# A third stream in chunks of 768 tokens, one product of 384 columns at a time, and a last product by token parity

## The chip, the cores and the metric

The kernel runs on one core of a Trainium2 chip. The metric is the device time of one execution in microseconds; of several runs, the median is taken.

## The reference, cut to what matters

Three layers follow each other over 8 batches of 576 tokens (4608 tokens, 512 features):

```python
# 1: attention with positive features, 8 heads of 64
proj = x @ w_phi; proj -= max(abs(proj)); phi = concat(exp(proj), exp(-proj))
out = (phi(q) @ (phi(k).T @ v)) / (phi(q) @ phi(k).sum() + 1e-6)
...
# 2: four experts, each a causal softmax attention over its batch; the two best per token are mixed
ye = softmax(scale * (x @ wq[e]) @ (x @ wk[e]).T, causal) @ (x @ wv[e]) @ wo[e]
...
# 3: mixing with the token before, then two products and a gate
xk = mu_k * x + (1 - mu_k) * x_prev;  xr = mu_r * x + (1 - mu_r) * x_prev
v = square(relu(xk @ w_k)) @ w_v
out = sigmoid(xr @ w_r) * v
```

`w_k` is 512 by 1024, `w_v` 1024 by 512, `w_r` 512 by 512.

## The kernel before

Everything is float32. Each product is made of three products of rounded parts (`mm3`: high by high, high by low, low by high), so that each operand has a `hi` and a `lo` tile (`split`, lines 94 to 99).

Work is written as streams (Python generators) of small tasks. `skewed` staggers the stages of successive tasks, and `weave` merges the streams by a clock of their own: the stream whose clock is lowest goes next, and a task adds its cost divided by the stream's rate. A task may have a condition; until it holds, the stream is passed over. The compiler's planner then orders the instructions of each engine by a simulated time and by priority; the streams `rk`, `compose` and `decodes` run at a lower priority (`-1000`) and so serve as filler.

- `favors` (first stream) is layer 1. For each of 160 pairs of token tiles it loads `raw`, splits it (`hi` on ScalarE, `lo` on GpSimd), makes `pj`, exponentials `ph`, the sums `kv`, the quotients `num`, and stores the result transposed in `XT`.
- `moe1` (second stream) is layer 2: `qk`, `vp`, scores `sc`, softmax `a`, transposes `at`, values `yp`. For each batch and pair of experts (`ep`) it stores its taps with `yd<-yt` (line 632). `stored[b]` is 2 when both pairs of a batch are issued.
- `compose` multiplies the output weights of layer 2 into `w_r` and `w_k` of layer 3 (12 blocks), so that layer 3's first products are taken straight from the taps; it leaves the weights in DRAM as `wf`. Products use even and odd tokens apart: a product of half tokens (`m`) serves both parities, and the products of slices 1 and 2 are added to it.
- `gates_keys` (third stream, `rk`) goes over the 4608 tokens in 9 chunks of `CH` = 512. A chunk loads its taps into `yc_` (one buffer, tag `y`), on ScalarE's queue; its condition is that the last batch that it touches is stored, that `compose` is done, and for the last two chunks that the second stream is over. Then 18 units follow: unit u has two products of 256 columns (12 matmuls) into one bank `rk`; every third one is copied to `m` by ScalarE, the others are added to `m` by VectorE into `z` (line 736) and stored to `kd`. Weights come as tiles `wt` of 512 KB, in three buffers, loaded on ScalarE's queue by `lw(n)`; after unit u the load for u+2 is issued. Until the first stream ends, all units share one bank; then two banks alternate.
- `moe2` (last product) goes over the same chunks: it loads pairs of blocks of `kd` (`kx`), applies relu and square, splits them into `XT` (free by then), and multiplies them with `w_v` into four banks `vacc` (24 matmuls of 512 columns per pair). `zs` is the gate (sigmoid). `fin` multiplies both into `o`, interleaving the two parities, and stores `out`. The first two `kx` have buffers of their own, the others lie in memory that the second stream frees when it ends.

When the second stream ends, a second `weave` (line 829) merges what is left of `rk` with `moe2`.

Of the kernel before, what the change touches and what calls it, by code (L numbers as in the profile page):

```python
# [13 lines left out]
P = 128  # L14
# [6 lines left out]
CH = 512  # L21
# [3 lines left out]
HC = CH // 2  # L25
NB = 18
# [48 lines left out]
def fused_kernel(ctx: ExitStack, tc: tile.TileContext, qT, kT, vx, wphi, wq, wk, wvg, wo, mu, w64, ident, cmask, tri, out):  # L75
# [12 lines left out]
    wf = [dram.tile([P, 2, 4, P], F32, name=f'wf{u}') for u in range(NB)]  # L88
    kd = [dram.tile([P, 12, CH], F32, name=f'kd{c}') for c in range(NC_)]

# [117 lines left out]
    def compose():  # L208
# [6 lines left out]
        for u in range(12):  # L215
            wth, wtl = (pR.tile([P, 4, 2, P], F32R, name=n, tag='w', bufs=3) for n in ('wth', 'wtl'))
            for hf in range(2):
                hz = (yield from decode(pF, 2 * u + hf, dict(tag='e', bufs=3), 2, 3, pool_raw=pR))
                ks = slice(2 * hf, 2 * hf + 2)
# [4 lines left out]
                split(wth[:, ks, 0], wtl[:, ks, 0], hz, 'a', nc.gpsimd)  # L224
                yield 1
                split(wth[:, ks, 1], wtl[:, ks, 1], a_, 'a', nc.gpsimd)
                yield 1
            ps = psK.tile([P, 512], F32, name='fo', tag='rk')
            for ep in range(2):
                es = slice(ep * P, ep * P + P)  # L230
                mm3(ps[:, ep * 256:ep * 256 + 256], [(sw[:, 0, kt, es], sw[:, 1, kt, es], wth[:, kt].rearrange('p x n -> p (x n)'), wtl[:, kt].rearrange('p x n -> p (x n)')) for kt in range(4)])
                yield 1
# [33 lines left out]
    def favor(b):  # L266
        kvbank = {}

        def proj_stages(src, g, u, dst, first=False):
# [98 lines left out]
        def q_unit(g, u):  # L368
# [17 lines left out]
            def num():  # L386
# [10 lines left out]
                dn = pF.tile([P, 2, 2], F32, name='dn', tag='dn', bufs=3)  # L397
                rd = pF.tile([P, 2, 2], F32, name='rd', tag='rd', bufs=3)
# [28 lines left out]
    def moe1():  # L427
# [168 lines left out]
        def av_task(b, e, hf):  # L596
# [72 lines left out]
    def favors():  # L669
# [17 lines left out]
        for f in range(8):  # L687
            s_ = pW.tile([P, 2 * CH], F32, name='wst2', tag='wst2', bufs=2)[:, :512]
# [16 lines left out]
    def gates_keys():  # L705

        def one(c):
# [3 lines left out]
            def ld():  # L711
                d['y'] = pR.tile([P, 2, 2, 3, HC], F32R, name='yc_', tag='y')
                load_y(c, d['y'], nc.scalar)
                if c == 0:
                    for n in range(3):
                        lw(n)

            def unit(u):

                def mm():  # L720
                    ps = psK.tile([P, CH], F32, name='rk', tag='kv' if 'favored' in state and u % 2 else 'rk')
                    w = wts.pop((c, u))
                    y = d['y']
                    for x in range(2):
                        sl = 0 if u % 3 == 0 else 1 + x
                        mm3(ps[:, x * HC:(x + 1) * HC], [(w[:, 0, 2 * x + ep], w[:, 1, 2 * x + ep], y[:, 0, ep, sl], y[:, 1, ep, sl]) for ep in range(2)])
                    d['p', u] = ps
                    return 1440

                def ev():  # L730
                    if u % 3 == 0:
                        d['m'] = pR.tile([P, 2, HC], F32, name='m1', tag='e', bufs=3)
                        evac('a', d['m'], d['p', u].rearrange('p (u t) -> p u t', u=2))
                    else:
                        z = pR.tile([P, 2, HC], F32, name='z', tag='e', bufs=3)
                        nc.vector.tensor_add(z, d['p', u].rearrange('p (w t) -> p w t', w=2), d['m'][:, u % 3 - 1].unsqueeze(1).to_broadcast([P, 2, HC]))  # L736
                        nc.sync.dma_start(kd[c][:, u // 3 * 2 + u % 3 - 1], z.rearrange('p w t -> p (w t)'))
                    lw(NB * c + u + 2)
# [138 lines left out]
```

## Time and profile before

| | before |
|---|---|
| median of 3 runs | 1355.43 us (1352.9 to 1356.6) |
| profiled execution, its own time | 1355.23 us |
| its span | 1352.6 us |
| mean granted clock of TensorE | 0.975 |
| TensorE busy | 1270.8 us (94%) |
| VectorE, ScalarE, GpSimd busy | 893.7, 743.4, 440.4 us |

The span is the time from the first to the last instruction of the profiled execution; its own time has some 2.6 us around it. A busy TensorE is one with a matmul in flight, so a matmul that waits for nothing but runs at the lower clock counts as busy. The granted clock is a share of full speed; at 0.5 the clock is 1.2 GHz instead of 2.4.

### The profile page before, as it was taken

Reading aid. Unit: us, or ns where it says so; the run is one execution under the profiler, and the core shown is the slowest. Engines: PE = TensorE matmul, PEld = TensorE weight load, DVE = VectorE, ACT = ScalarE, POOL = GpSimd, SP = SyncE. Lnnn points to the kernel's source line nnn. Section 1 sums busy time; section 2 is a strip of 40 time slices with the busy share of each in tenths; the row PEclk is TensorE's granted clock in tenths of the full one; section 3 lists DMA queues with packets and bytes.
Section 4 is the critical chain, followed back from the end, with each engine's and each line's share of the span. In section 5 each row is a group of like instructions: output and inputs, shape, how many; then the busy total and the mean of one; then the engine's idle time right before and its main releaser. Section 6 shows DMA issues by size and latency. Waiting matters only on the chain.

```text
span 1352.6 us, 26082 instructions
## 1 busy us (share of the span) xinstructions
PE 1270.8 (94%) x9000; PEld 1136.0 (84%) x9000; DVE 893.7 (66%) x2469; ACT 743.4 (55%) x1820; POOL 440.4 (33%) x602
## 2 busy tenths in 40 slices
PE   7999899989999999999999999888888869989998
PEld 5888788877998988898899899778787758878886
DVE  5876977987678777768787767556576444423542
ACT  5665756776557556656665656454445355323430
POOL 5543555753334433524452531312113100000000
PEclk8999999999999999999999999889998979989999
DMA  6342224225355454536353663687667898888641
GB/s 177 85 120 71 89 85 125 93 88 188 116 177 156 126 184 133 179 99 228 118 194 102 203 196 110 217 255 257 227 210 248 277 311 283 287 282 308 197 146 62
DMA packets 134738, 237.03 MB, mean 175 GB/s; under 512 B 21584, under 2 KB 75216, under 8 KB 134608
## 3 DMA queue, kind: packets, MB, share of 16 engines
q1 hardware_dynamic: 86192, 136.27, 30.4%
q10 hardware_dynamic: 48416, 99.10, 23.9%
q8 instruction: 72, 1.18, 0.4%
q14 instruction: 58, 0.48, 0.1%
HBM read 171.89 MB, written 63.44 MB: 174 GB/s over the span
## 4 chain that ended last, share of the span: by engine, by line
PE 77%; DVE 9%; DMA 8%; ACT 2%; issue 2%; POOL 1%; ACTq 1%; SPq 0%; POOLq 0%; DVEq 0%
PE rk L116 16%; PE vacc L116 13%; PE kv L343 9%; PE num L395 8%; PE qk L116 6%; PE vp L116 4%; DMA wt<-wf 3%; PE at L576 3%; PE yp L611 3%; PE pj L291 2%; PE pj L292 2%; PE pj L293 2%; PE sc L537 2%; PE tq L379 2%; PE sc L538 2%
## 5 line engine op out<-in xcount | busy, mean ns | idle before, releaser
L99 POOL TENSOR_TENSOR lo<-raw,hi 128x256 fp32r<-128x256 f32 (+1 forms) x160 | 110.0, 689 | 226.9 <-ACT hi L96 201.1
L116 PE MATMUL vacc<-XT,wvh 128*128 128x512 f32 x576 | 182.2, 395 | 0.0
L569 POOL TENSOR_SCALAR a<-a,rc,gw 128x128 f32<-128x128 f32 (+4 forms) x160 | 106.8, 670 | 171.0 <-DVE rc L563 65.0
L395 PE MATMUL num<-kvs,ph 128*128 128x65 f32 (+1 forms) x1280 | 147.2, 262 | 1.7 <-DVE xs L402 0.7
L395 PEld LDWEIGHTS num<-kvs,ph 128*128 128x128 f32 (+1 forms) x1280 | 139.1, 181 | 7.6 <-ACT ph L381 1.8
L736 DVE TENSOR_TENSOR z<-rk,m 128x512 f32<-128x512 f32 x108 | 74.1, 686 | 97.0 <-PE rk L116 74.6
L116 PEld LDWEIGHTS vacc<-XT,wvh 128*128 128x128 f32 x576 | 107.2, 188 | 24.0
L557 ACT ACTIVATE a<-sc,nm 128x128 f32<-128x128 f32 (+2 forms) x192 | 98.2, 514 | 41.6 <-DVE nm L551 20.9
L301 DVE TENSOR_REDUCE m<-pj 128x4 f32<-128x512 f32 (+1 forms) x160 | 100.8, 631 | 27.8 <-PE pj L293 26.8
L116 PE MATMUL vacc<-XT,wvl 128*128 128x512 f32 x288 | 112.9, 395 | 0.0
L291 PE MATMUL pj<-wph,hi 128*128 128x256 f32 x288 | 93.2, 323 | 13.2 <-DVE pm L303 4.9
L303 DVE TENSOR_TENSOR pm<-pj,m 128x512 f32<-128x512 f32 (+1 forms) x160 | 100.1, 628 | 1.8
L551 DVE TENSOR_REDUCE nm<-sc 128x1 f32<-128x128 f32 (+2 forms) x192 | 87.7, 468 | 6.3 <-PE sc L538 5.1
L782 ACT ACTIVATE kx<-kx 128x1024 f32<-128x1024 f32 x36 | 37.8, 1057 | 86.3 <-DMA kx<-kd 54.2
L293 PE MATMUL pj<-wph,lo 128*128 128x256 f32 x288 | 82.5, 287 | 0.7 <-POOL lo L99 0.7
L292 PE MATMUL pj<-wpl,hi 128*128 128x256 f32 x288 | 82.3, 286 | 0.0
L592 ACT ACTIVATE at1h<-at 128x384 fp32r<-128x384 f32 (+3 forms) x128 | 53.6, 420 | 51.5 <-PE at L576 39.4
L576 PE MATMUL at<-idn,a 128*128 128x128 f32 (+2 forms) x480 | 74.9, 266 | 5.2 <-POOL a L569 3.4
L96 ACT ACTIVATE hi<-raw 128x256 fp32r<-128x256 f32 (+1 forms) x160 | 62.7, 393 | 26.8 <-PE pj L292 20.0
L537 PE MATMUL sc<-k,qs 128*128 128x128 f32 (+2 forms) x192 | 68.6, 363 | 8.9 <-ACT a L557 8.8
L291 PEld LDWEIGHTS pj<-wph,hi 128*128 128x128 f32 x288 | 55.4, 192 | 18.6 <-ACT hi L96 4.9
L593 DVE TENSOR_TENSOR at1l<-at,at1h 128x384 fp32r<-128x384 f32 (+3 forms) x128 | 59.4, 464 | 13.8 <-ACT at1h L592 12.9
(516 smaller groups left out, 3468.7 us busy)
## 6 DMA issues: line engine op xcount, KB each, us to landing
wt<-wf ACTq DMA_DIRECT2D x162, 512.0 KB, 4.4
kd<-z SPq DMA_DIRECT2D x108, 256.0 KB, 4.4
kx<-kd SPq DMA_DIRECT2D x36, 512.0 KB, 4.5
yd<-yt SPq DMA_DIRECT2D x16, 864.0 KB, 5.5
zs<-kd SPq DMA_DIRECT2D x18, 512.0 KB, 6.1
out_dram<-o SPq DMA_DIRECT2D x36, 256.0 KB, 4.1
raw<-in_kT_dram SPq DMA_DIRECT2D x64, 128.0 KB, 2.4
raw<-in_qT_dram SPq DMA_DIRECT2D x64, 128.0 KB, 2.6
```

Source lines behind the costliest of these rows:

```text
L99: (el or nc.vector).tensor_sub(lo, src, hi.bitcast(F32))
L116: nc.tensor.matmul(ps, a, m, start=first and i == 0, stop=last and i == n - 1)
L291: nc.tensor.matmul(o, hi[:, c], wph, start=True, stop=False)
L292: nc.tensor.matmul(o, hi[:, c], wpl, start=False, stop=False)
L293: nc.tensor.matmul(o, lo[:, c], wph, start=False, stop=True)
L301: nc.vector.tensor_reduce(m[:, :g], ps, axis=AX.X, op=OP.max, apply_absolute_value=True)
L303: nc.vector.tensor_sub(pm[:, :g * P].rearrange('p (g f) -> p g f', f=P), ps, m[:, :g].unsqueeze(2).to_broadcast([P, g, P]))
L343: nc.tensor.matmul(bank[:, j, :], d['v'][:, i + (lo_ > 0), j, :], d['kp'][:, :, c0:c0 + P], start=new and j == 0, stop=end, skip_group_che ...
L395: nc.tensor.matmul(ps[lo_:hi_, i, j, :], d['qp'][:, hf, c0 + lo_:c0 + hi_], kvs[hp, b][:, r * 65:(r + 1) * 65], start=hf == 0, stop=hf == 1)
L557: nc.scalar.activation(a[:m, k0:k1_], o, AF.Exp, bias=nm[:m, 0:1], scale=1.0, accum_out=sm[:m, n:n + 1])
L569: eng(asc).tensor_scalar(a[:m, :nk], a[:m, :nk], rc[:m], WT[b][:m, i, e:e + 1], op0=OP.mult, op1=OP.mult)
L576: nc.tensor.transpose(ps[:kw, jj * m:jj * m + m], d['a'][:m, jj * P:jj * P + kw], idn[:m, :m])
```

## The change

The third stream takes 6 chunks of 768 tokens. A unit is one product of 384 columns (6 matmuls), and there are 36 of them per chunk. A weight tile holds one slice (256 KB, two pieces of 1 KB per partition), in five buffers, and after unit n the load for n+4 is issued. `compose` stores each block with one DMA and uses four half tiles. Only the last chunk now waits for the end of the second stream. The last product handles the 384 even tokens of a chunk and then the odd ones; `kd` is laid out by parity, `o` collects both parities and is stored after the second. To make room, `raw`, `dn`, `rd` and `xs` lose a buffer each, and `yc` moves into the ring of `a`. In the second `weave` the third stream starts 17000 behind.

```diff
-CH = 512
+CH = 768
...
-NB = 18
+NB = 36
+NWB = 5
...
-    wf = [dram.tile([P, 2, 4, P], F32, name=f'wf{u}') for u in range(NB)]
-    kd = [dram.tile([P, 12, CH], F32, name=f'kd{c}') for c in range(NC_)]
+    wf = [dram.tile([P, 2, 3, 2, P], F32, name=f'wf{u}') for u in range(12)]
+    kd = [dram.tile([P, 12, 2, HC], F32, name=f'kd{c}') for c in range(NC_)]
...
-            wth, wtl = (pR.tile([P, 4, 2, P], F32R, name=n, tag='w', bufs=3) for n in ('wth', 'wtl'))
+            wth, wtl = ([pR.tile([P, 2, 2, P], F32R, name=n, tag='w', bufs=NWB) for _ in range(2)] for n in ('wth', 'wtl'))
...
-            q3 = 3 * (u // 2)
-            nc.sync.dma_start(wf[q3][:, :, 2 * (u % 2):2 * (u % 2) + 2], o[:, :, 0].bitcast(F32))
-            nc.sync.dma_start(wf[q3 + 1 + u % 2], o[:, :, 1:].rearrange('p h x e n -> p h (x e) n').bitcast(F32))
+            nc.sync.dma_start(wf[u], o.bitcast(F32))
...
-                t_ = pF.tile([P, 256], F32, name='raw', tag='raw', bufs=3)
+                t_ = pF.tile([P, 256], F32, name='raw', tag='raw', bufs=2)
...
-                xs = pF.tile([P, 2, 2, 64], F32, name='xs', tag='xs', bufs=2)
+                xs = pF.tile([P, 2, 2, 64], F32, name='xs', tag='xs', bufs=1)
...
-                yc = pA.tile([64, 320], F32, name='yc', tag='yc', bufs=1)
+                yc = pA.tile([64, 320], F32, name='yc', tag='a', bufs=3)
...
-                    for n in range(3):
+                    for n in range(NWB):
                         lw(n)
 
-            def unit(u):
+            def unit(n):
+                u, sl = divmod(n, 3)
 
                 def mm():
-                    ps = psK.tile([P, CH], F32, name='rk', tag='kv' if 'favored' in state and u % 2 else 'rk')
-                    w = wts.pop((c, u))
+                    ps = psK.tile([P, 512], F32, name='rk', tag='kv' if 'favored' in state and n % 2 else 'rk')[:, :HC]
+                    w = wts.pop((c, n))
                     y = d['y']
-                    for x in range(2):
-                        sl = 0 if u % 3 == 0 else 1 + x
-                        mm3(ps[:, x * HC:(x + 1) * HC], [(w[:, 0, 2 * x + ep], w[:, 1, 2 * x + ep], y[:, 0, ep, sl], y[:, 1, ep, sl]) for ep in range(2)])
-                    d['p', u] = ps
-                    return 1440
+                    mm3(ps, [(w[:, 0, ep], w[:, 1, ep], y[:, 0, ep, sl], y[:, 1, ep, sl]) for ep in range(2)])
+                    d['p', n] = ps
+                    return 1040
 
                 def ev():
-                    if u % 3 == 0:
-                        d['m'] = pR.tile([P, 2, HC], F32, name='m1', tag='e', bufs=3)
-                        evac('a', d['m'], d['p', u].rearrange('p (u t) -> p u t', u=2))
+                    z = pR.tile([P, HC], F32, name='z', tag='e', bufs=3)
+                    if sl == 0:
+                        d['m'] = z
+                        evac('a', z, d['p', n])
                     else:
...
+                        nc.vector.tensor_add(z, d['p', n], d['m'])
+                        nc.sync.dma_start(kd[c][:, u, sl - 1], z)
-                    lw(NB * c + u + 2)
+                    lw(NB * c + n + NWB - 1)
...
-            return [[(lambda: stored.get(last, 0) == 2 and 'composed' in state and (c < 7 or 'late' in state), ld)]] + [[None]] + [unit(u) for u in range(NB)] + [[None]]
+            return [[(lambda: stored.get(last, 0) == 2 and 'composed' in state and (c < NC_ - 1 or 'late' in state), ld)]] + [[None]] + [unit(n) for n in range(NB)] + [[None]]
...
-                w = pR.tile([P, 2, 4, P], F32R, name='wt', tag='w', bufs=3)
-                nc.scalar.dma_start(w.bitcast(F32), wf[n % NB])
+                w = pR.tile([P, 2, 2, P], F32R, name='wt', tag='w', bufs=NWB)
+                u, sl = divmod(n % NB, 3)
+                nc.scalar.dma_start(w.bitcast(F32), wf[u][:, :, sl])
...
-        def chunk(c):
+        def chunk(c, par, os):
             t0 = c * CH
             d = {}
+            m = 2 * c + par
...
-                    d['z', g] = late['pB'].tile([P, 2, CH], F32, name='zs', tag='zs', bufs=4)
-                    nc.sync.dma_start(d['z', g], kd[c][:, 2 * g:2 * g + 2])
+                    d['z', g] = late['pB'].tile([P, 2, HC], F32, name='zs', tag='zs', bufs=4)
+                    nc.sync.dma_start(d['z', g], kd[c][:, 2 * g:2 * g + 2, par])
...
-                            d['v'] = [late['psB'].tile([P, CH], F32, name='vacc', tag=f'va{dt}') for dt in range(4)]
+                            d['v'] = [late['psB'].tile([P, 512], F32, name='vacc', tag=f'va{dt}')[:, :HC] for dt in range(4)]
...
-                        return 2720
+                        return 2070
...
-                        o = late['pB'].tile([P, CH], F32, name='o', tag='o', bufs=3)
-                        nc.vector.tensor_mul(o.rearrange('p (t two) -> p two t', two=2), *(x.rearrange('p (two t) -> p two t', two=2) for x in (d['v'][dt], d['z', dt // 2][:, dt % 2])))
-                        nc.sync.dma_start(out[P * dt:P * dt + P, t0:t0 + CH], o)
+                        if par == 0:
+                            os[dt] = late['pB'].tile([P, CH], F32, name='o', tag='o', bufs=6)
+                        nc.vector.tensor_mul(os[dt].rearrange('p (t two) -> p two t', two=2)[:, par], d['v'][dt], d['z', dt // 2][:, dt % 2])
+                        if par:
+                            nc.sync.dma_start(out[P * dt:P * dt + P, t0:t0 + CH], os[dt])
...
-    weave(tc, (fs, 0.0, 1.0, lambda: 0), (rk, 0.0, 1.0, lambda: 0), (m2, 0.0, 1.2, lambda: 0))
+    weave(tc, (fs, 0.0, 1.0, lambda: 0), (rk, 17000.0, 1.0, lambda: 0), (m2, 0.0, 1.0, lambda: 0))
```

## Rows read from the trace of the kernel before

**Rows 1.** Page, part 1: busy us, share of span, instructions.
```profile
PE 1270.8 (94%) x9000; PEld 1136.0 (84%) x9000; DVE 893.7 (66%) x2469; ACT 743.4 (55%) x1820; POOL 440.4 (33%) x602
```

**Rows 2.** By stages: busy PE, PEld, DVE, ACT, POOL; PEclk, DMA share, GB/s.
```profile
0.00:325.00 325.00, 298.52 (x2173) 259.50 (x2174) 258.89 (x745) 213.39 (x557) 175.62 (x248) 0.98 0.36 108
325.00:436.00 111.00, 110.89 (x878) 102.06 (x877) 84.03 (x251) 70.75 (x193) 44.25 (x61) 1.00 0.50 160
436.00:880.00 444.00, 434.96 (x3425) 402.00 (x3423) 325.44 (x986) 268.07 (x714) 176.79 (x237) 0.99 0.51 160
880.00:1085.00 205.00, 179.71 (x1279) 163.94 (x1279) 119.90 (x362) 94.34 (x260) 43.76 (x57) 0.94 0.76 247
1085.00:1256.00 171.00, 154.76 (x856) 134.84 (x856) 66.73 (x82) 71.39 (x75) 0.00 (x0) 0.94 0.85 287
```

**Rows 3.** Idle time of TensorE from 880 to 1085: us, times, longest.
```profile
PE rk L116 <- DMA wt<-wf: 10.9, 10, 2.1
...
PE rk L116 <- DVE z L736: 3.0, 2, 2.2
```

**Rows 4.** Matmuls into `rk`, by chunk: ns min/median/max, first and last start.
```profile
L116 PE MATMUL rk<-yc__5705,wt x216: 274/283/472, 325.8 to 484.4; 128*128 128x256 f32 x108
...
L116 PE MATMUL rk<-yc__13186,wt x216: 277/283/562, 889.1 to 942.3; 128*128 128x256 f32 x108
```

**Rows 5.** Pieces of the chain that ended last: start us, us, what.
```profile
1215.56 2.88 PE rk L116 x24
...
1255.57 90.31 PE vacc L116 x387
```

**Rows 6.** DMA issues from 880 to 1075: count, KB each, median us to landing.
```profile
wt<-wf ACTq DMA_DIRECT2D x55, 512.0 KB, 4.9
kd<-z SPq DMA_DIRECT2D x36, 256.0 KB, 4.8
```

**Rows 7.** A DMA issue between 436 and 500, same columns.
```profile
w__6817<-in_w_dram SPq DMA_DIRECT2D x1, 256.0 KB, 2.7
```

**Rows 8.** DMA queues: q1 in 0 to 325, q10 in 1200 to 1250.
```profile
q1 hardware_dynamic: 27696, 32.68, 33.4%
...
q10 hardware_dynamic: 1948, 7.06, 44.5%
```

**Rows 9.** Issuing instructions: duration ns min/median/max, first and last start.
```profile
L750 ACTq DMA_DIRECT2D wt<-wf x162: 326/326/2117, 295.2 to 1242.9; - x162
...
L632 SPq DMA_DIRECT2D yd<-yt x16: 524/525/593, 252.9 to 1075.1; - x16
```

**Rows 10.** All engines in order of time, 1083 to 1098: start, us.
```profile
1084.75 0.40 PE L116 MATMUL vacc<-XT,wvl 128*128 128x512 f32 x1
...
1085.37 0.80 SPq L779 DMA_DIRECT2D kx<-kd  x2
...
1094.20 1.23 DVE L99 TENSOR_TENSOR XT<-kx,XT 128x1024 fp32r<-128x1024 f32 x1
...
1097.94 0.58 PE L116 MATMUL rk<-yc__16039,wt 128*128 128x256 f32 x1 [7.55 <-DMA yc__16039<-yd]
```

**Rows 11.** TensorE in order of time, around 1190.
```profile
1188.02 0.40 PE L116 MATMUL vacc<-XT,wvl 128*128 128x512 f32 x1
...
1192.62 4.91 PE L116 MATMUL rk<-yc__16593,wt 128*128 128x256 f32 x22 [4.21 <-DMA yc__16593<-yd]
```

**Rows 12.** Stores of `yt` on SP in order of time: start us, us.
```profile
422.57 0.52 SPq L632 DMA_DIRECT2D yd<-yt  x1
...
1016.23 0.52 SPq L632 DMA_DIRECT2D yd<-yt  x1
```

**Rows 13.** Page part 5: the eviction L736, busy us, mean ns, idle before.
```profile
L736 DVE TENSOR_TENSOR z<-rk,m 128x512 f32<-128x512 f32 x108 | 74.1, 686 | 97.0 <-PE rk L116 74.6
```

**Rows 14.** VectorE at 384 columns: busy us, mean ns, idle before.
```profile
L593 DVE TENSOR_TENSOR at1l<-at,at1h 128x384 fp32r<-128x384 f32 x32 | 17.5, 546 | 2.8 <-ACT at1h L592 2.7
```

**Rows 15.** What SP's queue waited for up to 880: us, times, longest.
```profile
SPq L276 <- POOL lo L99: 323.3, 131, 8.2
```

More of the change, by code (lines that the diff above doesn't have):

```diff
@@ L230, in compose @@
                 es = slice(ep * P, ep * P + P)
-                mm3(ps[:, ep * 256:ep * 256 + 256], [(sw[:, 0, kt, es], sw[:, 1, kt, es], wth[:, kt].rearrange('p x n -> p (x n)'), wtl[:, kt].rearrange('p x n -> p (x n)')) for kt in range(4)])
+                mm3(ps[:, ep * 256:ep * 256 + 256], [(sw[:, 0, kt, es], sw[:, 1, kt, es], wth[kt // 2][:, kt % 2].rearrange('p x n -> p (x n)'), wtl[kt // 2][:, kt % 2].rearrange('p x n -> p (x n)')) for kt in range(4)])
                 yield 1
@@ L687, in favors @@
         for f in range(8):
-            s_ = pW.tile([P, 2 * CH], F32, name='wst2', tag='wst2', bufs=2)[:, :512]
+            s_ = pW.tile([P, 768], F32, name='wst2', tag='wst2', bufs=2)[:, :512]
             for j in range(2):
@@ L774, in ld @@
                 def ld():
-                    if 4 * c + p < 2:
-                        d['s', p] = late['pW'].tile([P, 2, CH], F32, name='kx', tag='wst2', bufs=2)
-                    else:
-                        d['s', p] = late['pB'].tile([P, 2, CH], F32, name='kx', tag='kx', bufs=5)
-                    nc.sync.dma_start(d['s', p], kd[c][:, 4 + 2 * p:6 + 2 * p])
+                    if 4 * m + p < 2:
+                        d['s', p] = late['pW'].tile([P, 2 * HC], F32, name='kx', tag='wst2', bufs=2).rearrange('p (u t) -> p u t', u=2)
+                    else:
+                        d['s', p] = late['pB'].tile([P, 2, HC], F32, name='kx', tag='kx', bufs=6)
+                    nc.sync.dma_start(d['s', p], kd[c][:, 4 + 2 * p:6 + 2 * p, par])
                 def ev():
@@ L783, in ev @@
                     nc.scalar.activation(d['s', p], d['s', p], AF.Square)
-                    n = (4 * c + p) % 4
-                    h_ = XT[:, (4 + n) * 1024:(5 + n) * 1024].rearrange('p (u t) -> p u t', u=2)
-                    l_ = XT[:, n * 1024:(n + 1) * 1024].rearrange('p (u t) -> p u t', u=2)
+                    n = (4 * m + p) % 6
+                    h_, l_ = (XT[:, (6 * i + n) * 768:(6 * i + n + 1) * 768].rearrange('p (u t) -> p u t', u=2) for i in range(2))
                     split(h_, l_, d['s', p])
@@ L805, in fin @@
                     for dt in range(4):
-                        o = late['pB'].tile([P, CH], F32, name='o', tag='o', bufs=3)
-                        nc.vector.tensor_mul(o.rearrange('p (t two) -> p two t', two=2), *(x.rearrange('p (two t) -> p two t', two=2) for x in (d['v'][dt], d['z', dt // 2][:, dt % 2])))
-                        nc.sync.dma_start(out[P * dt:P * dt + P, t0:t0 + CH], o)
-                return [(lambda: done.get(c, 0) == NB and B - 1 in read and len(wv2) == 2 and (4 * c + p < 2 or 'pB' in late), ld), None, None, ev, None, (lambda: 'pB' in late, vmm(0)), vmm(1), fin]
+                        if par == 0:
[3 more added lines that the diff above has]
+                            nc.sync.dma_start(out[P * dt:P * dt + P, t0:t0 + CH], os[dt])
+                return [(lambda: done.get(c, 0) == NB and B - 1 in read and len(wv2) == 2 and (4 * m + p < 2 or 'pB' in late), ld), None, None, ev, None, (lambda: 'pB' in late, vmm(0)), vmm(1), fin]
             return ([gate(g) for g in range(2)], [kt_(p) for p in range(4)])
@@ L812, in moe2 @@
         for c in range(NC_):
-            g, ks = chunk(c)
-            tasks += ks + g
+            os = {}
+            for par in range(2):
+                g, ks = chunk(c, par, os)
+                tasks += ks + g
         return skewed(tasks)
```

12 lines of the change are left out of this document (4 added, 8 removed).

## The prediction

> **What bounds the kernel now.** I read the page first: TensorE is busy 1270.8 of 1352.6 us [rows 1], so only its idle or slow stretches can be won, unless its work shrinks. The stretches by stage tell where these are [rows 2]. Up to 880 us TensorE is nearly full (from 325 to 880 it idles 9.1 of 555 us) and VectorE is its partner at three quarters. From 880 to 1085 it idles 25.3 of 205 us, at a mean granted clock of 0.94, with the DMA engines at 0.76: here the first stream is over, and the second one (attention) and the third (products into `rk`) alternate. From 1085 to 1256 it idles 16.2 of 171 us; after that it is full to the end.
>
> The waits of 880 to 1085 say what it idles for: mostly the weight tiles `wt` of the third stream, 10.9 us in 10 waits, then evictions of `rk`, 3.0 us in 2 [rows 3]. The stream as such is slower than that shows. Its chunk from 889.1 to 942.3 takes 53.2 us for 18 units, 2.96 us each [rows 4], while a unit's 12 products stream in 1.43 us (24 in 2.88, so 119.6 ns each at 256 columns, the last one's drain set aside) [rows 5]. The reason is the lead: the load for unit u+2 is issued after unit u, so two units can't be shorter than one landing, 4.9 us in this stretch [rows 6], and one unit's products, 1.43: 6.3 us, or 3.2 a unit.
>
> **The change, part by part.**
>
> *Products.* `rk` goes from 1944 matmuls of 256 columns to 1296 of 384, the last product from 864 of 512 to 1152 of 384; the columns stay. The trace has 119.6 ns at 256 and 90.31/387 = 233.4 ns at 512 [rows 5], 0.4445 ns a column, so 176.5 at 384. `rk`: 232.5 to 228.7 us; last product: 201.6 to 203.3. **-2.1 us**; no row at 384 in a dense series, bounds -4 to 0.
>
> *Weights.* 162 loads of 512 KB become 216 of 256 KB; five buffers let the load of unit n+4 be issued after unit n. Four units then cover one landing and one unit (6 x 176.5 = 1.06 us). The landing of 256 KB is 4.8 us in the crowded stretch [rows 6] and 2.7 in a quiet one [rows 7]: (4.8+1.06)/4 = 1.46 us a unit, or 0.94, which is below 1.06, so TensorE sets it. I take 1.46, as the stretch stays crowded: 768 tokens in 36 x 1.46 = 53 us instead of 27 x 2.96 = 80. The 10 waits go: **-10.9 us** (bounds 0 and -10.9). With them goes part of the half-clock time: 0.06 x 205 = 12.3 us of clock are missing in that stage [rows 2]; waits are some two fifths of its idle time, and I take a third of the clock, **-4 us** (0 to -12.3).
>
> Against this speaks that each row of a load now has two pieces of 1 KB in place of one of 4 KB. Packets of mean 1.18 KB took 0.334 x 16 x 325 us / 27696 = 62.7 ns, those of mean 3.62 KB 0.445 x 16 x 50 / 1948 = 183 ns [rows 8]: 18.8 and 19.8 bytes per ns, so a small piece costs some 5% more a byte, against a third fewer bytes (85 to 57 MB). The Trainium skill, "DMA: Bandwidth & Descriptors", section "Bandwidth", speaks the other way: it says to batch DMAs to 1 MiB or more for three quarters of the peak, and this change halves them. By that rule alone the weight term would be nothing and the time some 15 us longer; the packet rows do not bear it out.
>
> *Gaps between chunks.* The `y` tile has one buffer, so the stream stops while it is reloaded. In 880 to 1085 there are now two such gaps in place of two to three, each with half as many bytes again: **-3 us** of TensorE idle, 0 to -6, an estimate from that stage's 25.3 idle minus the waits named (11.4 left for gaps and softmax).
>
> *The hand-over at 1085.* Before, TensorE runs out of prepared tiles at 1085.1. The loads of further `kx` are issued at 1085.4, when the attention pool is free, and VectorE has the second of the next tiles split at 1095.4, the first 2 us sooner; but TensorE's queue has products into `rk` at its head, which wait for the `y` load until 1097.9 [rows 10]. After, the last product gets 17000 of head start in the planner, so it stands ahead of `rk`, and with three quarters of the columns a tile its next operand is ready at about 1093. But the two prepared tiles hold 8.5 instead of 11.2 us of products. Net -2.2; left-over units of the fifth chunk may fill the rest (-12.4). I take **-5 us**.
>
> *One chunk instead of two after the hand-over.* The second reload is gone: TensorE waited 4.2 us for it and then ran 22 products in 4.91 us, 2.1 more than at full clock [rows 11]. **-6.3 us** (0 to -6.3).
>
> *First chunk later.* 768 tokens need batch 1, whose last store is issued at 422.6 [rows 12]; with its landing and a reload, 12.5 us at the hand-over [rows 10], the stream starts at about 438 instead of 325.8 [rows 4]. That is 112 of the first chunk's 159 us, 112/159 x 25.8 = 18.2 us of products moved back. If TensorE without them is filled as in 0 to 325 (91.9% instead of 99.9% [rows 2], of which the start-up is a part), it loses up to 9 us; where the others advance instead, nothing. **+6 us**, 0 to +18. The later chunks wait for batches 2, 3, 5 and 6; the last of these is stored from 1016.2 [rows 12], before which the old kernel's seventh chunk could not begin either.
>
> *Evictions and queues.* `z` at 512 columns is 686 ns [rows 13], at 384 as 546 [rows 14]: 74 to 79 us of VectorE, behind TensorE. The 54 more issues on ScalarE are 326 ns each if their two pieces cost nothing, 525 for all 216 if they cost what a store in pieces costs [rows 9]: 18 to 61 us over 740, on an engine at 64% in 325 to 436 [rows 2]. 0, hidden by that slack; if it is gone, +5 through late exponentials. SP has 36 more `kd` stores, 18 more loads, 24 fewer `out` and `wf` issues: 30 of some 0.33 us [rows 9], also 0.
>
> *Fewer buffers.* SP already waits for `raw` to come free 131 times, 323 us in all [rows 15]; with two buffers in place of three it waits for the split of a unit nearer, and `kd` and `yd` stores queue behind it. TensorE's 9 us of idle time in 325 to 880 [rows 2] bound what such loads cost it now, so I take 0, at most another +5. `dn`, `rd`, `xs` and `yc` in `a`'s ring: their readers stand ahead in the engines' order; 0. The closing stores are 384 instead of 256 KB, but come from six buffers, not three: 0, within 1 either way.
>
> Sum: -2.1 -10.9 -4 -3 -5 -6.3 +6 = **-25.3 us**. The profiled execution took 1355.2 us, 2.6 more than its span and 0.2 under the median, so **1330**.
>
> **The rivals.**
>
> *No gain in the tail.* Attention's own chain (scores, softmax, transposes) sets 1085, and the faster third stream just waits for its batch. For it: batch 6 is stored only at 1016 [rows 12], and 11.4 us of idle time aren't weight waits. Against: the weight waits stand at the head of TensorE's queue and hold attention up too. Then weights, clock, gaps and hand-over give nothing: 1355.2 -2.1 -6.3 +6 = 1353.
>
> *Slower: the one bank.* Before the first stream ends, all units share one `rk` bank, so each unit waits for the eviction of the one before; there are 108 units before 880 or so where there were 72. An exposed turn costs 1.5 us (3.0 in 2 [rows 3]). It decides from 17 exposed turns on (25.3/1.5); with one in four, 27, the time is 1330 + 40 = 1370. Against: from 436 to 880 TensorE idles only 9 of 444 us, so turns are filled today.
>
> *More.* Filler is so plentiful that stage 880 to 1085 runs full (25.3 + 12.3), the hand-over is covered (12.4), the start costs nothing: 1355.2 - 37.6 - 12.4 - 6.3 - 2.1 = 1297; half of the extra over the forecast is 1313.
>
> **How the numbers follow.** Less than 0.3%, 4 us, can't be told from no change here. Forecast 0.53 (own range 1316 to 1345), no gain 0.18, slower 0.14, more 0.15. Faster: 0.53 + 0.15 + a quarter of the no-gain case, 0.72; same 0.14; slower 0.14. The range runs to 1306, inside "more", and to 1362, the near half of "slower".
>
> **What would show it.** In the profile after: `rk` at 176 ns a product; units 1.1 to 1.6 us apart where dense; TensorE's wait for `wt` near nothing; 57 MB of weights; first `rk` at about 438; one `y` wait after the hand-over; the idle time in the stage before it under 15 us. Wrong would make it: TensorE's idle time before 880 growing by more than 15 us (the first chunk, the bank), ScalarE becoming the releaser of scores and transposes, or landings that stay at 4.9 us or more with half the bytes.

## The result: 20 us faster, and where the time came from

The changed kernel takes 1337.22 us in the median of 4 runs (1329.92 to 1339.88), the kernel before 1356.01 in 4 runs beside it: ratio 0.9853 [0.9825, 0.9881], so 16 to 24 us less (the medians differ by 18.8). The profiled execution took 1339.02 us, 1.8 above its median; against the profiled one of before the spans differ by 15.4 us, and this is the sum that the traces have to explain.

The page of the changed kernel, its span and part 1, answers to [rows 1]:

```profile
span 1337.2 us, 25714 instructions
...
PE 1273.3 (95%) x8640; PEld 1168.5 (87%) x8640; DVE 897.9 (67%) x2541; ACT 750.4 (56%) x1868; POOL 442.4 (33%) x602
```

TensorE is busy 2.5 us longer in a span that is 15.4 us shorter: idle time went, not busy time. By stages, with the columns of [rows 2]:

```profile
0.00:325.00 325.00, 296.68 (x2102) 258.05 (x2103) 252.52 (x723) 203.44 (x536) 170.94 (x241) 0.96 0.32 99
325.00:436.00 111.00, 106.04 (x794) 92.36 (x793) 82.52 (x254) 75.94 (x202) 48.42 (x67) 1.00 0.33 102
436.00:880.00 444.00, 438.62 (x3215) 403.52 (x3214) 320.62 (x978) 261.43 (x705) 165.74 (x226) 0.99 0.48 142
880.00:1070.00 190.00, 172.99 (x1049) 157.24 (x1048) 126.99 (x404) 102.27 (x282) 54.09 (x66) 0.92 0.70 216
1070.00:1085.00 15.00, 15.00 (x93) 14.58 (x92) 6.80 (x16) 5.65 (x14) 3.23 (x3) 1.00 0.88 277
1085.00:1256.00 171.00, 168.14 (x961) 167.25 (x960) 78.13 (x124) 82.85 (x110) 0.00 (x0) 1.00 0.84 271
```

Idle time grew from 26.6 to 33.3 us before 436 and fell from 9.0 to 5.4 in 436 to 880, from 25.3 to 17.0 in 880 to 1085 and from 16.2 to 2.9 in 1085 to 1256, where the clock rose from 0.94 to 1.00.

Fixed times compare different work once the kernels have drifted apart. A marker that both have serves better: the first and the last store of `yt`, which bound the second stream's output. Before they are issued at 252.9 and 1075.1 [rows 9]; after:

```profile
L630 SPq DMA_DIRECT2D yd<-yt x16: 524/525/605, 266.7 to 1083.4; - x16
```

Stretches between these markers, columns as in [rows 2], first before, then after:

```profile
0.00:252.90 252.90, 232.34 (x1682) 201.40 (x1682) 197.26 (x555) 162.64 (x417) 133.38 (x191) 0.98 0.36 107
252.90:1075.10 822.20, 781.84 (x6028) 718.37 (x6029) 591.00 (x1788) 483.91 (x1304) 307.05 (x412) 0.98 0.55 176
1075.10:1352.60 277.50, 256.62 (x1292) 216.27 (x1290) 105.42 (x128) 96.87 (x99) 0.00 (x0) 0.96 0.70 236
```

```profile
0.00:266.70 266.70, 243.38 (x1711) 211.58 (x1711) 202.22 (x569) 164.03 (x426) 134.14 (x193) 0.96 0.33 101
266.70:1083.40 816.70, 784.35 (x5525) 712.58 (x5526) 587.23 (x1804) 484.70 (x1310) 308.29 (x411) 0.97 0.50 153
1083.40:1337.20 253.80, 245.59 (x1406) 244.38 (x1404) 108.41 (x170) 101.69 (x132) 0.00 (x0) 1.00 0.69 225
```

So the start lost 13.8 us, the middle won 5.5 and the end won 23.7: together -15.4. Of the loss at the start, 29 matmuls (1711 against 1682) are work done earlier, some 4 us at the 142 ns that one takes on average there (243.38/1711). 2.8 us are more idle time (23.3 instead of 20.6), and the other 7 are busy time that no further matmul accounts for, at a granted clock of 0.96 instead of 0.98. At the end the same two streams are left, and a little less of them: 270 matmuls into `rk` at 175.8 ns in place of 432 at 119.6, and 1136 into `vacc` at 173.4 in place of 860 at 233.4, 244.5 us in place of 252.4 (after: 2.11/12 and 92.41/533 in the chain below). Of the other 15.8 us of the 23.7, 12.7 are idle time that is gone; some 3 go with the clock, 1.00 instead of 0.96.

The forecast had nothing for the start. Its worst 50 us, before and after, columns as in [rows 2]:

```profile
150.00:200.00 50.00, 45.09 (x340) 39.63 (x339) 42.72 (x127) 30.57 (x83) 29.31 (x41) 0.97 0.29 89
```

```profile
150.00:200.00 50.00, 43.23 (x291) 39.65 (x291) 36.75 (x114) 25.11 (x72) 22.24 (x32) 0.83 0.22 70
```

All engines are less busy (TensorE's weight loads as much as before). TensorE idled 1.9 us more and was granted 0.83 of the clock instead of 0.97: 49 matmuls fewer in the same stretch. No third stream runs here yet, so the smaller rings of the first stream and the recut weight tiles of `compose` come into question. The recut tiles alone do little: the run of units alone, below, has them with the old rings, and stores its first `yt` at 255.2, 2.3 us after the kernel before.

The third stream itself: waits of TensorE from 880 to 1083 (us, times, longest), against [rows 3]; DMA issues there, against [rows 6]; the first and the fifth chunk, against [rows 4]; two pieces of the chain that ended last, against [rows 5]:

```profile
PE sc L535 <- ACT a L555: 6.9, 5, 2.4
PE rk L117 <- ACT z L104: 3.9, 4, 2.9
PE at L574 <- POOL a L567: 3.8, 5, 1.6
PE rk L117 <- DVE z L733: 1.8, 4, 1.0
```

```profile
wt<-wf ACTq DMA_DIRECT2D x83, 256.0 KB, 3.9
kd<-z SPq DMA_DIRECT2D x56, 192.0 KB, 3.5
```

```profile
L117 PE MATMUL rk<-yc__6068,wt x216: 331/337/527, 442.1 to 621.2; 128*128 128x384 f32 x108
...
L117 PE MATMUL rk<-yc__15287,wt x216: 333/336/452, 1037.9 to 1132.6; 128*128 128x384 f32 x108
```

```profile
1217.69 2.11 PE rk L117 x12
...
1237.89 92.41 PE vacc L117 x533
```

The weight waits are gone from TensorE. VectorE, however, has a new one: before, its evictions `z` waited 2.5 us in all for a store to `kd` to land; now it is 20.8 (whole run, us, times, longest; first before, then after):

```profile
DVE z L736 <- DMA kd<-z: 2.5, 2, 2.2
```

```profile
DVE z L733 <- DMA kd<-z: 20.8, 14, 7.0
```

The hand-over, TensorE in order of time (start us, us), against [rows 10]:

```profile
1088.52 0.34 PE L117 MATMUL vacc<-XT,wvl 128*128 128x384 f32 x1
1088.69 2.27 PE L117 MATMUL rk<-yc__15287,wt 128*128 128x384 f32 x12
1092.28 2.38 PE L117 MATMUL rk<-yc__15287,wt 128*128 128x384 f32 x12 [1.32 <-ACT z L104]
1094.50 0.86 PE L117 MATMUL vacc<-XT,wvh 128*128 128x384 f32 x4
```

When the prepared tiles are used up at 1088.7, units of the fifth chunk, whose `y` is long loaded, fill the time until the next tile at 1094.5. One wait of 1.3 us stands where there were two, the 7.6 us for `y` and, just before it, one in which TensorE waited for nothing that the profile shows:

```profile
PE rk L116 <- issue: 4.5, 1, 4.5
```

### The profile page after: what moved, and what is told of

Its sections match the earlier page's. It is cut to its first block, busy times and chain, and to the rows that moved or that the text cites. A ratio compares the mean times of both kernels' runs of the same rounds, so it can differ in the third digit from the quotient of the medians.

```text
span 1337.2 us, 25714 instructions
## 1 busy us (share of the span) xinstructions
PE 1273.3 (95%) x8640; PEld 1168.5 (87%) x8640; DVE 897.9 (67%) x2541; ACT 750.4 (56%) x1868; POOL 442.4 (33%) x602
## 4 chain that ended last, share of the span: by engine, by line
PE 57%; DMA 4%; DVE 3%; ACT 1%; issue 1%; POOL 1%; ACTq 0%; POOLq 0%; DVEq 0%; SPq 0%
PE rk L117 15%; PE vacc L117 14%; PE qk L117 5%; PE num L393 4%; PE kv L341 4%; PE vp L117 3%; PE at L574 2%; PE yp L609 2%; PE sc L535 2%; DMA kd<-z 1%; PE sc L536 1%; PE pj L289 1%; PE pj L290 1%; PE tq L377 1%; PE pj L291 1%; DMA wt<-wf 1%
## 5 line engine op out<-in xcount | busy, mean ns | idle before, releaser
L117 PE MATMUL vacc<-XT,wvh 128*128 128x384 f32 x768 | 195.9, 336 | 1.5 <-DVE o L806 1.5
L117 PEld LDWEIGHTS vacc<-XT,wvh 128*128 128x128 f32 x768 | 138.9, 188 | 1.9 <-DVE o L806 1.9
L733 DVE TENSOR_TENSOR z<-rk,z 128x384 f32<-128x384 f32 x144 | 79.7, 553 | 83.7 <-PE rk L117 40.3
L117 PE MATMUL vacc<-XT,wvl 128*128 128x384 f32 x384 | 127.6, 336 | 0.0
L299 DVE TENSOR_REDUCE m<-pj 128x4 f32<-128x512 f32 (+1 forms) x160 | 100.6, 630 | 24.8 <-PE pj L291 23.7
L535 PE MATMUL sc<-k,qs 128*128 128x128 f32 (+2 forms) x192 | 69.1, 365 | 10.9 <-ACT a L555 10.7
L117 PEld LDWEIGHTS vacc<-XT,wvl 128*128 128x128 f32 x384 | 72.0, 188 | 0.0
L781 ACT ACTIVATE kx<-kx 128x768 f32<-128x768 f32 x48 | 40.1, 842 | 55.8 <-DMA kx<-kd 45.3
```

The source lines that it names most:

```text
L117: nc.tensor.matmul(ps, a, m, start=first and i == 0, stop=last and i == n - 1)
L299: nc.vector.tensor_reduce(m[:, :g], ps, axis=AX.X, op=OP.max, apply_absolute_value=True)
L535: nc.tensor.matmul(o, q_[:, j, qs], k1[:, j, ks], start=True, stop=False)
```

## The experiments

Two theories stood at first. The weight theory: the gain comes from the weight loads, which no longer hold back the units. The hand-over theory: it comes from there, and the units themselves win little.

**Units alone.** The kernel before with the small units, still in chunks of 512 tokens with the old last product (36 units of one product of 256 columns; `compose` is recut to match).

```diff
-NB = 18
+NB = 36
+NWB = 5
...
-                w = pR.tile([P, 2, 4, P], F32R, name='wt', tag='w', bufs=3)
+                w = pR.tile([P, 2, 2, P], F32R, name='wt', tag='w', bufs=NWB)
...
-                    lw(NB * c + u + 2)
+                    lw(NB * c + n + NWB - 1)
```

> The kernel before (chunks of 512, old last product, old second weave) with the units alone changed: 36 units of one product of 256 columns, weight tiles of 256 KB in five buffers, loaded four units ahead. Weights theory (my sum): the ten waits for weights between 880 and 1085 go, some 15 us faster than before, about 1340, less if 1728 more issues and 256-column evictions cost. Rival (the gain sits at the hand-over, where this kernel is unchanged): TensorE finds other waits in the same stage, within 5 us of before. By either, TensorE's waits for wt fall under 3 us.

1405.73 us, ratio 1.0362 [1.033, 1.0395]: 50 us **slower**. TensorE's weight waits are gone here, too (from 880 to the end):

```profile
PE rk L117 <- DMA wt<-wf: 0.7, 2, 0.4
```

So the weight theory falls as it stood. VectorE's waits, and the stretch from the last store of `yt` (1056.1) to the end:

```profile
DVE z L733 <- PE rk L117: 84.1, 49, 9.4
DVE z L733 <- DMA kd<-z: 46.4, 31, 4.0
```

```profile
1056.10:1402.60 346.50, 306.93 (x1567) 260.13 (x1565) 120.04 (x184) 103.85 (x127) 0.00 (x0) 0.94 0.73 240
```

Attention ended 19 us sooner than before, but 720 matmuls into `rk` were left instead of 432. The third stream fell behind as filler, and the end took 69.0 us longer, of which 288 x 119.6 ns = 34.4 are the work left over. The hand-over itself is covered even so: 12 units of a loaded chunk are left (720 matmuls, less three chunks of 216, by 6), and from 1050 to 1100 TensorE has one wait, and none for `y`:

```profile
PE vacc L117 <- DVE XT L99: 2.3, 1, 2.3
```

**The second weave alone**, in the kernel before.

```diff
-    weave(tc, (fs, 0.0, 1.0, lambda: 0), (rk, 0.0, 1.0, lambda: 0), (m2, 0.0, 1.2, lambda: 0))
+    weave(tc, (fs, 0.0, 1.0, lambda: 0), (rk, 17000.0, 1.0, lambda: 0), (m2, 0.0, 1.0, lambda: 0))
```

> The kernel before with the second weave alone changed: the third stream 17000 behind, the last product at rate 1.0. Hand-over theory: TensorE's 12 us stop after 1085 shrinks, but two chunks and two reloads are still to come and no left-over units fill it: 3 to 8 us faster than before. Rival (the stop is filled only by left-over units of a chunk that is already loaded): within 3 us of before, the stop stays at 8 us or more.

1355.03 us, 0.9984 [0.9965, 1.0003]: no change. TensorE's order of matmuls is that of the kernel before up to 1119 us, so the head start does not reach the hand-over, and the stop is still there:

```profile
1094.21 4.63 PE L116 MATMUL rk<-yc__16140,wt 128*128 128x256 f32 x20 [7.64 <-DMA yc__16140<-yd]
```

**The first chunk's condition alone**: it names batch 1 in the kernel before.

```diff
-            return [[(lambda: stored.get(last, 0) == 2 and 'composed' in state and (c < 7 or 'late' in state), ld)]] + [[None]] + [unit(u) for u in range(NB)] + [[None]]
+            return [[(lambda: stored.get(max(last, 1), 0) == 2 and 'composed' in state and (c < 7 or 'late' in state), ld)]] + [[None]] + [unit(u) for u in range(NB)] + [[None]]
```

> The kernel before in which the first chunk also waits for batch 1, as 768 tokens make it do. My sum: 6 us slower (0 to 18), with more idle time of TensorE between 325 and 440. Rival (the other streams take the room at no loss and the third catches up): within 2 us of before.

1356.64 us, 0.9997 [0.9975, 1.0019], but the first matmul into `rk` still ran at 327.1, and TensorE's order of its 9000 matmuls is that of the kernel before throughout. The condition only orders the writing of the tasks; the planner placed them when their data was there. So this run says nothing about a late start.

**Fewer buffers alone**, in the kernel before.

```diff
-                t_ = pF.tile([P, 256], F32, name='raw', tag='raw', bufs=3)
+                t_ = pF.tile([P, 256], F32, name='raw', tag='raw', bufs=2)
...
-                xs = pF.tile([P, 2, 2, 64], F32, name='xs', tag='xs', bufs=2)
+                xs = pF.tile([P, 2, 2, 64], F32, name='xs', tag='xs', bufs=1)
...
-                yc = pA.tile([64, 320], F32, name='yc', tag='yc', bufs=1)
+                yc = pA.tile([64, 320], F32, name='yc', tag='a', bufs=3)
```

(`dn` and `rd` go from three to two as well.)

> The kernel before with the buffers of the change alone: two for raw, dn and rd, one for xs, and yc in the ring of a. My sum: no change, at most 5 us slower. Rival (the single xs holds VectorE and the products num and transposes xt behind it, which the profile after shows with 6.2 us of TensorE waits against 1.8 before): 4 to 10 us slower.

1363.51 us, 1.0054 [1.003, 1.0077]: 7 us lost, and the trace says where. The stores of `yt`:

```profile
L632 SPq DMA_DIRECT2D yd<-yt x16: 519/525/526, 262.4 to 1085.6; - x16
```

The first is 9.5 us late, the last 10.5, so the loss is made before the first store, as in the changed kernel (the end takes 4.3 us less). That the single `xs` does it by making TensorE wait is not borne out: its waits for `xs` are 1.8 us before, 4.9 here and 6.2 in the changed kernel, but 4.8 in the kernel with a fourth eviction tile (below), whose start isn't late. **`yc` alone** does none of it:

```diff
-                yc = pA.tile([64, 320], F32, name='yc', tag='yc', bufs=1)
+                yc = pA.tile([64, 320], F32, name='yc', tag='a', bufs=3)
```

> The kernel before with yc alone moved into the ring of a. If the cost of the fewer buffers sits there: 4 to 8 us slower than before, with TensorE's waits of scores for exponentials (8.8 us before) above 12. If it sits in raw and xs: within 2.5 us of before.

1354.94 us, 0.9986 [0.9967, 1.0005], the first store at 255.6. `raw`, `dn`, `rd` and `xs` are left; they were not taken apart one by one.

After these runs there was a third theory, that of the ring: dense units are paced by the ring of three eviction tiles `e`. A tile of it is free only when its store to `kd` has landed, and a halved unit takes a whole tile. With one tile for `m` and two for `z`, three units can't be shorter than a landing and an addition: before (4.8 + 0.69)/3 = 1.8 us a unit with 1.43 us of products, in the run of units alone (3.3, the landing that its trace shows for 128 KB, + 0.42)/3 = 1.24 with 0.72, after (3.5 + 0.55)/3 = 1.35 with 1.06. These are floors that the theory gives, not measured paces: the densest chunk of the run of units alone (1242.6 to 1307.5, 36 units) took 1.8 us a unit.

**Lead of two, after.** The changed kernel, its weight loads written two units ahead instead of four.

```diff
-                    for n in range(NWB):
+                    for n in range(3):
...
-                    lw(NB * c + n + NWB - 1)
+                    lw(NB * c + n + 2)
```

> The changed kernel, its weight loads issued two units ahead instead of four (five buffers stay). Weights theory: two units of 384 columns then take a landing of 3.9 us and 1.06, 2.5 us a unit where the third stream is dense, so the waits for weights come back: 10 us or more over the changed kernel's 1337. Rival (a ring theory: since the change, the ring of three eviction tiles z, each held until its store has landed, paces the dense units): within 4 us of the changed kernel.

1335.33 us, 0.9828 [0.9803, 0.9852]: as the changed kernel, and still no wait of TensorE for `wt` between 880 and 1083. But the loads did not go out later. Up to 985 us, first the changed kernel and then this run: weight loads issued, and busy time of the products into `rk` with their number (6 a unit).

```profile
L748 ACTq DMA_DIRECT2D wt<-wf x131: 525/526/1822, 323.8 to 984.9; - x131
...
0.00:985.00 985.00, 169.95 (x757) 128.92 (x757) 49.27 (x99) 20.53 (x42) 0.97 0.43 130
```

```profile
L748 ACTq DMA_DIRECT2D wt<-wf x132: 525/526/1669, 323.2 to 984.1; - x132
...
0.00:985.00 985.00, 169.42 (x766) 129.76 (x767) 49.84 (x100) 21.04 (x43) 0.98 0.43 131
```

126 and 127 units were complete, and the loads stood five ahead in both: a load goes out when one of the five buffers comes free, wherever it is written. (Taken one by one, it is issued 0.04 us in the median after the last product with the tile that it replaces, in either kernel.) So this run does not test the lead. The runs with four buffers, below, do shorten it, by one unit.

**Units alone with a fourth eviction tile.**

```diff
-                    z = pR.tile([P, HC], F32, name='z', tag='e', bufs=3)
+                    z = pR.tile([P, HC], F32, name='z', tag='e', bufs=4)
```

(The other two users of the tag have four then, too.)

> The kernel of the first experiment (the units alone, chunks of 512, 1405.7 us) with four eviction tiles instead of three. Ring theory: its loss of 50 us came from tiles of 256 columns that are each held some 4 us by their store, so one more tile gives back 15 to 30 us. Rival (the loss is from more units as such: 324 turns and issues): less than 8 us back.

1384.04 us, 1.0189 [1.0162, 1.0216]: 22 us come back (the profiled execution was the fastest of its runs, 1375.9 us). VectorE's waits for `kd` stores fall from 46.4 to 12.1 us. The stretch from the last store of `yt`, and what TensorE waits for from 880 on:

```profile
1049.60:1374.10 324.50, 293.62 (x1554) 249.35 (x1552) 119.36 (x182) 104.11 (x126) 0.00 (x0) 0.98 0.78 254
```

```profile
PE rk L117 <- DMA wt<-wf: 23.7, 17, 3.2
PE rk L117 <- DVE z L733: 8.3, 6, 3.5
```

22.0 us less in that stretch with nearly the same work left (702 matmuls against 720), and the next limit shows itself: the weight loads. So the ring theory holds for units of 256 columns, for 22 of the 50 us.

**The changed kernel with a fourth eviction tile** and, to make room, four weight buffers.

```diff
-NWB = 5
+NWB = 4
...
-                    z = pR.tile([P, HC], F32, name='z', tag='e', bufs=3)
+                    z = pR.tile([P, HC], F32, name='z', tag='e', bufs=4)
```

> The changed kernel with four eviction tiles z instead of three, paid for by four weight buffers instead of five (three units ahead). Ring theory: the 23.3 us for which VectorE and ScalarE wait for stores kd<-z (16 waits, 9.6 us of them on VectorE from 880 to 1084) fall under 8, and the time falls by 4 to 10 us to 1327 to 1333. Weights theory: lead of three, four units cost one landing in three, so the same or up to 4 us slower.

1330.09 us, 0.9795 [0.9767, 0.9822]: the fastest kernel of all, 7 us under the changed kernel's median, and VectorE has no wait for `kd` stores left. The profiled execution was its fastest, 1326.39 us, so the traces differ by more, 12.6 us. But the gain isn't where the ring theory puts it. The stores of `yt`, and the stretches between them:

```profile
L630 SPq DMA_DIRECT2D yd<-yt x16: 524/525/602, 253.8 to 1073.8; - x16
```

```profile
253.80:1073.80 820.00, 786.77 (x5567) 714.59 (x5567) 598.95 (x1814) 486.22 (x1317) 304.89 (x410) 0.98 0.51 153
1073.80:1324.60 250.80, 242.26 (x1388) 240.87 (x1386) 107.96 (x168) 101.69 (x131) 0.00 (x0) 1.00 0.68 225
```

The first store comes 12.9 us sooner than in the changed kernel, the middle takes 3.3 longer and the end 3.0 less. It wins the start back, 170 us before the first matmul into `rk` (424.3); `compose` decodes its weights in the same ring. What the evictions of `rk` win is 3 us at most, and the end has 18 matmuls fewer to do. Nor does the dense stretch of the third stream go faster: its fourth chunk, in the changed kernel and then here, takes 72.2 and 72.7 us.

```profile
L117 PE MATMUL rk<-yc__13637,wt x216: 331/336/446, 948.0 to 1020.2; 128*128 128x384 f32 x108
```

```profile
L117 PE MATMUL rk<-yc__13635,wt x216: 331/337/441, 932.4 to 1005.1; 128*128 128x384 f32 x108
```

So the ring of eviction tiles does not pace the units of 384 columns.

**raw and xs given back** to the changed kernel, with four weight buffers.

```diff
-NWB = 5
+NWB = 4
...
-                t_ = pF.tile([P, 256], F32, name='raw', tag='raw', bufs=2)
+                t_ = pF.tile([P, 256], F32, name='raw', tag='raw', bufs=3)
...
-                xs = pF.tile([P, 2, 2, 64], F32, name='xs', tag='xs', bufs=1)
+                xs = pF.tile([P, 2, 2, 64], F32, name='xs', tag='xs', bufs=2)
```

> The changed kernel with four weight buffers instead of five, and for it three raw and two xs again. Buffers theory (the fourth experiment: the fewer buffers cost 7.3 us, in the first stream's xs and raw): 3 to 7 us faster than the changed kernel, TensorE's 6.2 us of waits for xs under 3. Rival (the cost sits in yc in the ring of a): within 2 us of it.

1335.76 us, 0.9855 [0.9829, 0.9882]: no gain in the end, though the start is won back here as well:

```profile
L630 SPq DMA_DIRECT2D yd<-yt x16: 524/525/1093, 256.2 to 1085.3; - x16
```

The first store is 10.5 us sooner, the last 1.9 later. In between stand 31 matmuls that the changed kernel had done earlier, and weight waits that four buffers bring back (2.9 us in 4); the rest of these 12 us isn't attributed. `dn` and `rd` still have two buffers here, so they don't hold the start up by themselves. But both runs that win the start back also have four weight buffers instead of five, in a ring that `compose` uses as well; no run has that alone, so it isn't shown that the tiles given back do it.

**A late start that is one.** The kernel before with its first two chunks exchanged, so that the first needs batch 1 by its data.

```diff
+        pm_ = [1, 0] + list(range(2, NC_))
...
-                load_y(c, d['y'], nc.scalar)
+                load_y(pm_[c], d['y'], nc.scalar)
```

> The kernel before with its first two chunks swapped, so that the third stream can start only when batch 1 is stored, at about 438 instead of 326, by its data and not only by the order of writing. My sum: 6 us slower (0 to 18), TensorE idle for some 5 us more in 325 to 436. Rival: the other streams advance instead, within 2 us of before.

1355.5 us, 0.9976 [0.9953, 0.9999]. The first chunk ran from 425.8 to 543.3 instead of 325.8 to 484.4, the third ended at 781.9 instead of 772.6: a delay of 100 us was nearly made up by then and cost nothing.

**The old second weave**, in the changed kernel.

```diff
-    weave(tc, (fs, 0.0, 1.0, lambda: 0), (rk, 17000.0, 1.0, lambda: 0), (m2, 0.0, 1.0, lambda: 0))
+    weave(tc, (fs, 0.0, 1.0, lambda: 0), (rk, 0.0, 1.0, lambda: 0), (m2, 0.0, 1.2, lambda: 0))
```

> The changed kernel with the second weave of before: third stream at 0, last product at rate 1.2. Head-start theory (the sum's hand-over step): products into rk stand ahead of the last product on TensorE's queue again and wait for y, so the stop after 1083 comes back and costs 5 to 10 us over the changed kernel's 1337. Left-over theory (the nine units of the fifth chunk that are still to do, with weights and taps at hand, fill the stop whatever the order): within 4 us of the changed kernel.

1337.79 us, 0.9855 [0.9829, 0.9881]: the same time, with the end at 253.2 us. TensorE's order of matmuls is that of the changed kernel up to 1116 us, so the head start is not what covers the hand-over.

**The fifth chunk held back**, in the changed kernel.

```diff
-            return [[(lambda: stored.get(last, 0) == 2 and 'composed' in state and (c < NC_ - 1 or 'late' in state), ld)]] + [[None]] + [unit(n) for n in range(NB)] + [[None]]
+            return [[(lambda: stored.get(last, 0) == 2 and 'composed' in state and (c < NC_ - 2 or 'late' in state), ld)]] + [[None]] + [unit(n) for n in range(NB)] + [[None]]
```

> The changed kernel in which the fifth chunk, too, may only be written after the end of the second stream, so that two chunks follow the hand-over, as before the change. Left-over theory: attention's last 50 us lose their filler and a second reload stands after the hand-over: TensorE idles 10 to 25 us more and the time rises by as much, to 1347 to 1362. Rival (the gain came from before the hand-over): within 4 us of the changed kernel.

1337.99 us, 0.9871 [0.984, 0.9903]. But the planner began the fifth chunk at 1035.7 all the same (1037.9 in the changed kernel), and 8 of its units were left when attention ended: once more a condition held the writing back and not the work.

What covers the hand-over is seen best by laying all fourteen traces side by side. In the six kernels with the old units, no unit of a loaded chunk is left when attention ends, and TensorE then waits 7.5 to 8.0 us for `y`. In the eight with small units, 6 to 12 such units are left, and none waits for `y` there. Two of these eight, the runs of units alone with three and with four eviction tiles, have the old chunks, the old last product and the old weave. So, as far as these traces go, it is the left-over units that cover the hand-over; no run has small units without them.

## Why the prediction was right, and which of its steps were not

The time was forecast as 1330 and came to 1337, by -20 in place of -25.3. Direction and size stand; several terms don't, and that the sum came so near is in part luck. Between the markers the start took 13.8 us more, where nothing was forecast; the middle 5.5 less, where the waits, the clock, the gaps and the later first chunk were to make 11.9; the end 23.7 less, where the hand-over and the reload were to make 11.3. The errors cancel.

- **Fewer buffers, "0, at most another +5": the step that failed.** Alone they cost 7 us in the old kernel, and the start of the changed one is 13.8 us late (some 10 without the work done earlier). TensorE's idle time in 325 to 880 was taken as the bound; the cost lay before 267, with more idle time and a lower clock together. Two runs recover the start (12.9 with one more `e` tile, 10.5 with `raw` and `xs`), each with one weight buffer fewer; only the first of them is faster in all (0.9795 against 0.9853). Which ring does it, and how, is open.
- **Products, -2.1.** By the durations after (175.8 ns in `rk`, 173.4 in `vacc`; forecast 176.5) they give 232.5 to 227.8 and 201.6 to 199.8: -6.5, outside the bounds of -4 to 0.
- **Weights, -10.9, clock, -4, and gaps, -3: this step failed, too.** The waits did vanish, but the stretch from 880 to 1085 gave back 8.3 us of idle time, gaps included, not 13.9 (17.0 us are left, not under 15), and its clock gave nothing (0.94 before, 0.93 after). The forecast took the lead as it is written: the load for u+2 goes out after unit u. In the traces it goes out when a buffer comes free. In the kernel before, 84 loads are issued up to 915 us, when 972/12 = 81 units are complete, three ahead (loads, then products into `rk` with the columns of [rows 2], GpSimd left out):

```profile
L750 ACTq DMA_DIRECT2D wt<-wf x84: 326/326/1372, 295.2 to 915.0; - x84
...
0.00:915.00 915.00, 157.90 (x972) 131.41 (x972) 40.88 (x67) 16.07 (x27) 0.98 0.47 145
```

  With the landings measured, that makes three units a landing, by estimate (4.9 + 1.43)/3 = 2.1 us a unit where the forecast had 3.2, and with five buffers (3.9 + 1.06)/5 = 1.0 where it had 1.46. The fourth chunk took 72 us for 36 units (948.0 to 1020.2), 2.0 us each; the fifth did 27 units from 1037.9 to 1080.5, 1.6 each. So neither the weight loads nor the ring of eviction tiles (1.35) set this pace, and a fourth eviction tile left it as it was. TensorE's longest waits there are now for attention (6.9 and 3.8 us) and for an eviction by ScalarE (3.9); what sets the pace was not isolated.
- **Pieces of 1 KB.** Queue 10, which carries the loads of `wt` and `y`, moved, before and then after:

```profile
q10 hardware_dynamic: 48416, 99.10, 23.9%
```

```profile
q10 hardware_dynamic: 77568, 70.79, 18.7%
```

  That is 19.2 and 17.7 bytes per ns and engine (0.239 x 16 x 1352.6 us and 0.187 x 16 x 1337.2): a byte took 8% more of the queue's time, where the forecast had some 5%, and the queue is still busy 22% less of the span. The Trainium skill, "DMA: Bandwidth & Descriptors", section "Bandwidth", asks for batches of 1 MiB or more, by a table of DMAs issued from GpSimd; these are issued by ScalarE. The trace agrees in the direction, for a byte; whether the halved load or its shorter pieces cost it isn't separated. The kernel became faster all the same, and the queue moves 29% fewer bytes.
- **Hand-over, -5, and one reload less, -6.3.** Together -11.3; measured -12.7 of idle time after the last store (277.5 - 256.62 = 20.9 to 253.8 - 245.59 = 8.2), and some 3 more from the clock, 0.96 to 1.00. The size was right. The reason for the first part was the lesser one: it was laid on the head start, which in two runs leaves TensorE's order at the hand-over as it was; the "left-over units of the fifth chunk", named as an extra, are what the trace shows at 1088.7 and what sets the kernels without the stop apart.
- **First chunk later, +6.** The trace has 4.9 us of idle time more in 325 to 436, but a start 100 us later cost nothing in the old kernel, and 3.7 of them come back by 880.
- **Evictions on one bank, 0.** The rival of the one `rk` bank did not come: from 436 to 880 TensorE idles 5.4 us. ScalarE's issues take 525 ns each now, and among TensorE's waits from 880 to 1083 none names a weight load that was issued late.

What stays open is how the gain divides between the larger chunks, the smaller units and the last product by parity. The left-over units that cover the hand-over come with the small units, but units alone lose 50 us. The chunk of 768 (216 units instead of 324, two thirds of the weight bytes, one reload instead of two in the end) may carry the gain. That is argued, not shown: no run has the chunk without the units, the run of units alone has 256 columns a unit and not 384, and each edit moves the planner's whole order.

## What to carry to other kernels

A ring whose tiles are held until a store has landed limits a stream to tiles per landing: when units are cut smaller, count every ring that a unit passes through, not only the one that is being deepened, and expect the next ring to take over. Such a count gives a floor; look in the trace whether the stream comes near it. Compare kernels between events that both have, not between fixed times; that is how a loss of 14 us at the start was seen under a gain of 20. A condition in the order of writing doesn't hold back what a planner places by data, and a load written later need not go out later: an experiment on lateness has to change the data or the buffers, and the trace has to show that it did.

## What was not expected of the hardware

Landings don't go in proportion to size: weight loads took 4.9 us at 512 KB and 3.9 at 256. Stores to `kd` took 4.8 at 256 KB, 3.5 at 192 and only little less, 3.3, at 128. These are different kernels, in stretches where the DMA engines were at 0.7 to 0.76, so the size isn't isolated. And little idle time can stand beside a lot of slow time: from 150 to 200 us, 1.9 us more of it went with a granted clock of 0.83 in place of 0.97. The amount of idle time alone doesn't decide it: in the run with the first chunk's condition alone TensorE idled 6.0 us there, 1.1 more than before, and was granted the full clock.
